# First part of an expert begun inside the last attention blocks, and the last chunk routed block by block

## The chip, the cores and the metric

One core of a Trainium2 chip runs the kernel. The metric is the device time of one execution in microseconds (us); the kernel before has a median of 445.17 us over 3 runs. The engines are PE (TensorE, matrix products), DVE (VectorE), ACT (ScalarE), POOL (GpSimd) and SP (SyncE, which issues transfers). Each works through its own instructions in the order in which the program wrote them.

## The reference

The input is attention with a decaying state (4 batches, 8 heads, 768 steps, width 48), and its output goes through a layer of 8 experts, of which each token takes one:

```python
y[:, :, t] = einsum('bhd,bhde->bhe', rt, state + cur)      # cur = outer(u * kt, vt)
state = wt[:, :, :, None] * state + einsum('bhd,bhe->bhde', kt, vt)
x = y.transpose(0, 2, 1, 3).reshape(3072, 384)
expert_idx = argmax(x @ w_gate);  gate_w = softmax(x @ w_gate)[expert_idx]
for e in range(8):
    out[mask] = gate_w[mask, None] * (maximum(x[mask] @ w1[e], 0) @ w2[e])
```

## The kernel before, in words

**Attention.** The sequence is cut into 6 chunks of 128 steps, and chunk c of batch b is block n = 4c + b, so there are 24 blocks, 0 to 23. `iteration(n)` (L692) does for block n the products `pe_a` (k against r, tile `ap`), `pe_inter` (the state's part, into `yp`) and `pe_av` (values, into `yp`), prepares block n + 2 on DVE and ACT (`dve_suf`, `dve_kh`, `dve_pre`, `dve_rh`, `pe_coef`, `pe_coef_tr`) and finishes block n - 1 (`act_y`, `pe_y`, `act_xr`, which leave its rows in `xr`). `pe_coef` and `pe_state` begin with a few products of zeros, `keep_warm` (L108), whose results nobody reads; blocks 20 to 23 have no `pe_state`, and iterations 22 and 23 no `pe_coef`.

**Routing.** The logits of a chunk are computed, `gate` (L521, five small DVE operations) finds the expert, `count` adds up how many tokens each expert has, `rank` (L565, three small products for one block) and `place` (L581, three DVE operations) give each token its row, `weigh` the factor, and `scatter` (L647) is an indirect transfer on POOL's queue that stores the rows by expert in DRAM. Chunks 0 to 4 are routed whole, four blocks at a time, one chunk later. In the last chunk each block is routed alone (`pe_logits`, L596): its logits one iteration after its attention, gate at the end of that iteration, rank and place in the one behind it. `rank` of block n - 2 stands on PE between `pe_a(n)` and `pe_inter(n)` (L711).

**Experts.** An expert takes its rows (`load_rows`), transposes them (`transpose_rows`, L265), and for 8 groups f computes `expand` (L273: 9 products into a bank, then `hh` by ACT and `hl` by DVE), and then `contract` or the products of L872, 24 for each output tile. Expert 0 goes in two parts: `pa`, 192 rows that come from chunks 0 to 3 and are thus there early, and `pb`, 256 rows, whose load waits for every scatter. In the kernel before `pa` is loaded at the end of iteration 20, transposed at the end of iteration 22, its group 0 stands in iteration 23, and groups 1 to 7 behind, with the routing of blocks 22 and 23 between them. Then come `pa.mm2(0)`, `pb.trans`, `pa.mm2(1)`, the 8 groups of `pb` and the other experts.

**What sets the order.** It is written out by hand for PE, DVE, ACT and POOL (`manual_schedule`, L888), and for SP too. PSUM tiles come in rings: `psX` has 2 buffers (transposes, `rank`, and in the kernel before the single-block logits), `psL` 1 (`pe_coef`, `pe_coef_tr`), `psK` and `psA` 2 each. A new tile waits until those who read the tile two (or one) before it are done. `transpose_rows` takes three `psX` tiles, each read by ACT and then by DVE:

```python
for j in range(3):
    pt = psX.tile([P, nq * rows], F32, name="pt", tag="tp")
    ...
    nc.scalar.activation(xh[:, j, :], pt, AF.Copy)
    nc.vector.tensor_tensor(out=xl[:, j, :], in0=pt, in1=xh[:, j, :].bitcast(F32), op=ALU.subtract)
```

Of the kernel before, what the change touches and what calls it, by code (L numbers as in the profile page):

```python
# [19 lines left out]
P = 128  # L20
C = 128
NCH = S // C
# [23 lines left out]
def rwkv_moe_kernel(ctx, tc, rkw, vv, ub, wgp, wg, w1, w2, out):  # L46
# [192 lines left out]
    def scatter_out(t, q, rows):  # L239
# [3 lines left out]
        for k in outs:  # L243
# [1 line left out]
        outs.append(i.ins)  # L245

    banks = [(psK, "kp"), (psK, "kp"), (psY, "yp"), (psL, "lg")]
    htags = [("suf", "pre"), ("suf", "pre"), ("rk", "rk"), ("rk", "rk"), ("kh", "rh"), ("kh", "rh"), ("kh", "rh"),
             ("kt", "kt"), ("at",), ("at",)]
    nth = {"b": 0, "h": 0}  # L250

# [28 lines left out]
        nc.scalar.activation(hh, hp, AF.Relu)  # L280
        nc.vector.scalar_tensor_tensor(out=hl, in0=hp, scalar=0.0, in1=hh.bitcast(F32), op0=ALU.max, op1=ALU.subtract)  # L281

    def contract(wt, hs, q, rows, t):
        op = psA.tile([rows, DM], F32, name="opt", tag="ap")
        i = 0
        for f in range(8):
            hh, hl = hs[f]
            cs = slice(q * rows, (q + 1) * rows)
            for a, w in ((hh, "h"), (hl, "h"), (hh, "l")):
                nc.tensor.matmul(op, a[:, cs], w2v(wt, w, f), start=(i == 0), stop=(i == 23))  # L290
                i += 1
        o = ld.tile([rows, DM], F32, name="ort", tag="vt")
        nc.vector.tensor_scalar(out=o, in0=op, scalar1=t[:, q, DM:DM + 1], scalar2=None, op0=ALU.mult)
        scatter_out(t, q, o)
# [203 lines left out]
    def pe_y(n):  # L498
        if real(n):
            yq = psX.tile([P, NP_ * RP], F32, name="yq", tag="tp")  # L500
            for q in range(NP_):
                nc.tensor.transpose(yq[:, q * RP:(q + 1) * RP], blk[n]["yt"][:, q, :], ident[:RP, :RP])  # L502
            blk[n]["yq"] = yq
# [33 lines left out]
    def act_ex(k):  # L537
        ex = sm.tile([P, B, E], F32, name="ex", tag="ex")[:, 0:k[2]]
        nc.scalar.activation(ex, ch["r", k][0], AF.Exp)
        ch["ex", k] = ex  # L540
# [14 lines left out]
    def weigh(k):  # L555
        c, b, m = k
        se = sm.tile([P, B], F32, name="se", tag="se")[:, 0:m]
        nc.vector.tensor_reduce(out=se, in_=ch["ex", k], axis=AX.X, op=ALU.add)
        nc.vector.tensor_scalar(out=se, in0=se, scalar1=1e-9, scalar2=None, op0=ALU.add)
        nc.vector.reciprocal(ch["xr", c][:, b:b + m, DM], se)  # L560
# [4 lines left out]
    def rank(k):  # L565
        c, b, m = k
        oh = ch["r", k][1]
        oa = ch["old", k]
        rk = psX.tile([P, B + 1, E], F32, name="rank", tag="tp")
        ch["rank", k] = rk  # L570
        if c == ROUTED:
            nc.tensor.matmul(rk[:, B, :], ones, oa, start=True, stop=True, skip_group_check=True)
        rk = rk[:, 0:m, :]
        nc.tensor.matmul(rk, tri, oh, start=True, stop=False, skip_group_check=True)
        nc.tensor.matmul(rk, ones[0:1, :], ebrow[:, 0:m], start=False, stop=False, skip_group_check=True)
        nc.tensor.matmul(rk, ones, oa.unsqueeze(1).broadcast_to([P, m, E]), start=False, stop=(m == 1), skip_group_check=True)
        for i in range(m - 1):
            nc.tensor.matmul(rk[:, i + 1:m, :], ones, oh[:, i:i + 1, :].broadcast_to([P, m - 1 - i, E]),
                             start=False, stop=(i == m - 2), skip_group_check=True)
# [16 lines left out]
    def pe_logits(n):  # L596

        c, b = divmod(n, B)
        lg = psX.tile([P, 1, E], F32, name="lg", tag="tp")
        for q in range(NP_):  # L600
            nc.tensor.matmul(lg[:, 0, :], blk[n]["yt"][:, q, :], wgt[:, q, 0:E], start=(q == 0), stop=(q == NP_ - 1))
        ch["lp", (c, b, 1)] = lg
# [59 lines left out]
    class Part:  # L662
# [13 lines left out]
            expand(wt0, f, self.x[0], self.x[1], bank(2 * self.rows), hh, hl)  # L676
            self.hs.append((hh, hl))

        def mm2(self, q):
            contract(wt0, self.hs, q, self.rows, self.t)  # L680

    load_v(0)
    for n in range(1, LD):
# [8 lines left out]
    def iteration(n):  # L692

        c, b = divmod(n, B)
        route = c - 1 if n >= 0 else -1
        if n >= 0:
            load(n + 6)
            load_v(n + 5)
        last = c == NCH - 1
        whole = (route, 0, B)  # L700
        act_y(n - 1)
        pe_a(n)
        dve_suf(n + 2)
        act_g(n + 1)
        if route >= 0 and b == 1:
            act_ex(whole)
        pool_rk(n + 3)
        if n in (6, 7):
            scatter(0, (2 * n - 12,))
        if last and b > 1:  # L710
            rank((c, b - 2, 1))  # L711
        pe_inter(n)
        dve_at(n)
        dve_state(n - 1)
        pool_diag(n + 1)
        act_diag(n + 1)
        if n in (6, 7):
            scatter(0, (2 * n - 11,))
        if route > 0 and b > 1:
            scatter(route, (2 * b - 4, 2 * b - 3))  # L720
        if route >= 0 and b == 1:
            count(whole)
            weigh(whole)
        if n > 0 and b == 1:
            ch["xr", c] = xrp.tile([P, B, XC], F32, name="xr", tag="xr")
            pool_ids(c)
        if last and b > 1:
            act_ex((c, b - 2, 1))
            place((c, b - 2, 1))
            weigh((c, b - 2, 1))  # L730
        if last and b == 3:
            scatter(c, (0,))
        pe_y(n - 1)
        if last and b > 0:
            pe_logits(n - 1)
        if n == NB - 1:
            pa.mm1(0)
        dve_kh(n + 2)
        act_xr(n - 1)
        pe_coef(n + 2)  # L740
        act_cs(n + 2)
        if route >= 0 and b == 0:
            logit_mm(route)
        if route >= 0 and b == 1:
            rank(whole)
        pe_kt(n + 1)
        act_kt(n + 1)
        dve_pre(n + 2)
        if route >= 0 and b == 0:
            logit_tr(route)  # L750
        pe_state(n)
        pe_coef_tr(n + 2)
        act_ct(n + 2)
        act_wt(n + 2)
        dve_rh(n + 2)
        for k in lows:
            split_piece(*k, half="l")
        lows.clear()
        if route >= 0 and b == 0:
            gate(whole)  # L760
        if route >= 0 and b == 1:
            place(whole)
        if last and b > 0:
            gate((c, b - 1, 1))
            count((c, b - 1, 1))
        act_junk(n + 2)
        m = n - 8
        if 0 <= m < 12:
            lows.append((wt0, stg[0, m // 3], m // 3, 3, m % 3))
            split_piece(*lows[0], half="h")  # L770
        pe_av(n)
        if n == NB - 2:
            pa.trans()
        if n == 0:
            zero_rows()
        if n == 1:
            late_constants()
        if 1 <= n < 5:
            prefill(2 * n - 2)
            prefill(2 * n - 1)  # L780
        if n in (6, 9, 12, 15):
            stg[0, n // 3 - 2] = load_piece(one, n // 3 - 2)
        if n in (14, 17, 20, 21):
            stg[1, (14, 17, 20, 21).index(n)] = load_piece(SECOND, (14, 17, 20, 21).index(n))
# [101 lines left out]

    ET = mybir.EngineType
    with tc.manual_schedule(engines={ET.PE, ET.DVE, ET.Activation, ET.Pool}):  # L888
        for n in range(-3, NB):
            iteration(n)  # L890
            if n == 20:
                pa = Part(0, HA // 2)
                full, banks = banks, banks[0:2]

        nl = NB - 1
        mid, end = (NCH - 1, B - 2, 1), (NCH - 1, B - 1, 1)
        act_y(nl)
        banks = [(psA, "ap"), (psA, "ap"), (psK, "kp"), (psK, "kp")]
        pa.mm1(1)
        rank(mid)  # L900
        act_ex(mid)
        place(mid)
        weigh(mid)
        pe_y(nl)
        pe_logits(nl)
        scatter(NCH - 1, (1, 2))
        act_xr(nl)
        gate(end)
        act_ex(end)
        count(end)  # L910
        pa.mm1(2)
        pa.mm1(3)
        rank(end)
        place(end)
        weigh(end)
        scatter(NCH - 1, (3,))
        pa.mm1(4)
        sort_experts()
        check_w()
        pa.mm1(5)  # L920
        pa.mm1(6)
        check()
        actx.close()
        wpb = mctx.enter_context(tc.tile_pool(name="wpb", bufs=1))
        wts.append(weight_tiles(wpb))
        pa.mm1(7)
        split_piece(wts[1], stg[1, 0], 0)
        pb = Part(HA, HB // 2)
        load_x(1)
        expert(2)  # L930
        feed(1, 0, False)
        pa.mm2(0)
        pb.trans()
        split_piece(wts[1], stg[1, 1], 1)
        feed(1, 1, False)
        pa.mm2(1)
        banks = full
        nth["b"] = 0
        for f in range(8):
            pb.mm1(f)  # L940
            if f in (1, 4):
                feed(1, 2 + f // 4)
        pb.mm2(0)
        trans_x(1)
        pb.mm2(1)
# [203 lines left out]
```

## Time and profile before

| what | us |
|---|---|
| median of 3 runs (lowest, highest) | 445.17 (444.72, 447.03) |
| the profiled execution | 448.3 |
| its span, first to last instruction | 446.6 |
| PE busy | 420.1 (94%) |
| DVE, ACT, POOL busy | 285.4, 223.4, 125.5 |

The mean granted TensorE clock is 0.966 of full speed. All times below are from the span's start. A timeline's line gives start, length, engine, line and operation, out<-in tiles, sizes and, in brackets, how long the engine stood idle before it and what ended that. PE's lengths overlap a little, so what a group of products costs is read from one start to the next, as the chain of waits does.

### The profile page before, as it was taken

The numbers are of one execution on the slowest core, as the hardware profiler recorded it, in microseconds if no ns is written. First come the engines' busy times: TensorE is split into PE (matmuls) and PEld (weight loads), VectorE is DVE, ScalarE is ACT, GpSimd is POOL, SyncE is SP. The second block draws the span as 40 slices with busy tenths as digits, with TensorE's granted clock in tenths as the row PEclk, the third lists the DMA queues.
The fourth block names the chain that finished last, engine by engine and source line by source line (L and its number), as shares of the span: only waits on it lengthen the run. The fifth ranks groups of instructions, "written<-read, shape, count | busy, mean of one in ns | idle before, by whom it ended". The sixth has DMA issues, their size and how long they took to land.

```text
span 446.6 us, 9684 instructions
## 1 busy us (share of the span) xinstructions
PE 420.1 (94%) x3662; PEld 368.4 (82%) x3663; DVE 285.4 (64%) x554; ACT 223.4 (50%) x625; POOL 125.5 (28%) x159
## 2 busy tenths in 40 slices
PE   8989999999899979998999999999999999999990
PEld 6557778777677758897999988899999999999990
DVE  5899899999999994374875166165363572722310
ACT  3678787787786861232755244353353461522200
POOL 3663255451634523011010012022030080210710
PEclk9999999999999995598999999999999999999997
DMA  7999977776863152036572643544365335000120
GB/s 201 215 216 285 240 208 197 192 238 130 253 170 107 57 169 90 19 101 189 156 243 66 198 133 93 174 149 116 133 189 161 114 89 160 27 26 1 23 59 23
DMA packets 33179, 62.61 MB, mean 140 GB/s; under 512 B 8086, under 2 KB 21199, under 8 KB 33126
## 3 DMA queue, kind: packets, MB, share of 16 engines
q1 hardware_dynamic: 25222, 52.41, 42.4%
q0 software_dynamic: 7904, 9.52, 6.9%
q8 instruction: 30, 0.49, 0.5%
q14 instruction: 23, 0.19, 0.1%
HBM read 50.03 MB, written 12.29 MB: 140 GB/s over the span
## 4 chain that ended last, share of the span: by engine, by line
issue 38%; PE 33%; DVE 11%; ACT 6%; POOL 5%; DMA 3%; POOLq 0%; ACTq 0%; DVEq 0%
PE bank L278 7%; POOL out_dram L240 4%; DMA out_dram<-ot,xg 3%; PE bank L872 3%; PE opt L290 3%; PE yp L473 3%; PE wrm L111 2%; DVE at L364 2%; PE yp L495 2%; PE ap L461 2%; DVE pre L356 2%; DVE suf L340 2%; PE dp L486 2%; PE yq L502 2%; ACT junk L379 1%
## 5 line engine op out<-in xcount | busy, mean ns | idle before, releaser
L240 POOL DMA_INDIRECT out_dram<-ot,xg x24 | 35.3, 1470 | 156.9 <-DVE ot L862 151.4
L216 DVE TENSOR_TENSOR w2l<-wst,w2h 128x512 fp32r<-128x512 f32 x48 | 31.4, 685 | 44.6 <-ACT w2h L214 44.1
L278 PE MATMUL bank<-xl,w1h 128*128 128x448 f32 (+6 forms) x168 | 59.0, 355 | 0.0
L278 PE MATMUL bank<-xh,w1l 128*128 128x448 f32 (+6 forms) x168 | 58.2, 352 | 0.0
L278 PE MATMUL bank<-xh,w1h 128*128 128x448 f32 (+6 forms) x168 | 55.7, 359 | 0.4 <-issue 0.3
L312 POOL TENSOR_TENSOR rk<-rkwt 112x512 f32<-112x512 f32 x24 | 33.6, 1399 | 76.1 <-DVE pre L344 55.4
L281 DVE SCALAR_TENSOR_TENSOR hl<-bank,hh 128x192 fp32r<-128x192 f32 (+8 forms) x58 | 30.4, 539 | 32.4 <-ACT hh L280 32.2
L280 ACT ACTIVATE hh<-bank 128x192 fp32r<-128x192 f32 (+8 forms) x58 | 26.6, 477 | 46.7 <-PE bank L278 43.9
L872 PE MATMUL bank<-hl,w2h 128*128 128x412 f32 (+5 forms) x114 | 40.6, 358 | 0.0
L872 PE MATMUL bank<-hh,w2l 128*128 128x412 f32 (+5 forms) x114 | 40.5, 357 | 0.0
L877 ACT ACTIVATE oT<-bank 128x448 f32<-128x448 f32 (+5 forms) x18 | 9.4, 525 | 61.6 <-PE bank L872 61.6
L872 PE MATMUL bank<-hh,w2h 128*128 128x412 f32 (+5 forms) x114 | 39.9, 356 | 0.0
L650 POOL DMA_INDIRECT xs<-xr,pi x24 | 26.2, 1091 | 28.1 <-DVE sh L527 11.5
L364 DVE COPY_PREDICATED at<-cmask,ap 128x512 f32<-128x512 int32 x48 | 32.3, 727 | 2.7 <-PE ap L461 2.2
L340 DVE TENSOR_TENSOR_SCAN suf<-rkwt,sufone 112x520 f32<-112x520 f32 x24 | 31.1, 1296 | 4.2 <-DMA rkwt<-in_rkw_dram 4.2
L278 PEld LDWEIGHTS bank<-xh,w1h 128*128 128x128 f32 x168 | 31.2, 188 | 1.9 <-issue 0.5
L278 PEld LDWEIGHTS bank<-xl,w1h 128*128 128x128 f32 x168 | 31.6, 188 | 1.1
L278 PEld LDWEIGHTS bank<-xh,w1l 128*128 128x128 f32 x168 | 31.5, 188 | 1.1
L214 ACT ACTIVATE w1h<-wst 128x512 fp32r<-128x512 f32 x48 | 28.2, 628 | 8.1 <-PE bank L278 7.9
L216 DVE TENSOR_TENSOR w1l<-wst,w1h 128x512 fp32r<-128x512 f32 x48 | 30.9, 685 | 1.2 <-PE bank L278 0.6
L356 DVE TENSOR_TENSOR_SCAN pre<-rkwt,pre 112x520 f32<-112x520 f32 x24 | 31.1, 1295 | 0.0
L334 ACT ACTIVATE at<-ident,ct 128x128 f32<-128x128 f32 x96 | 30.5, 391 | 0.1
(163 smaller groups left out, 932.1 us busy)
## 6 DMA issues: line engine op xcount, KB each, us to landing
wst<-in_w_dram SPq DMA_DIRECT2D x48, 256.0 KB, 3.8
wst<-in_w_dram SPq DMA_DIRECT2D x16, 768.0 KB, 6.9
rkwt<-in_rkw_dram SPq DMA_DIRECT2D x36, 289.5 KB, 6.6
vt<-in_vv_dram SPq DMA_DIRECT2D x24, 192.0 KB, 5.7
rkwt<-in_rkw_dram SPq DMA_DIRECT2D x5, 675.5 KB, 16.8
xg<-xs SPq DMA_DIRECT2D x5, 579.0 KB, 4.4
xs<-zrow SPq DMA_DIRECT2D x8, 289.5 KB, 6.8
xg<-xs SPq DMA_DIRECT2D x2, 675.5 KB
```

What stands on the lines that cost most here:

```text
L214: nc.scalar.activation(hi, st[:, cs], AF.Copy)
L216: nc.vector.tensor_tensor(out=lo, in0=st[:, cs], in1=hi.bitcast(F32), op=ALU.subtract)
L240: i = nc.gpsimd.indirect_dma_start(out=out[:, :], out_offset=bass.IndirectOffsetOnAxis(ap=t.bitcast(I32)[:, q, DM + 1:DM + 2], axis=0), in ...
L278: nc.tensor.matmul(hp, a, x[:, j, :], start=(i == 0), stop=(i == 8))
L280: nc.scalar.activation(hh, hp, AF.Relu)
L281: nc.vector.scalar_tensor_tensor(out=hl, in0=hp, scalar=0.0, in1=hh.bitcast(F32), op0=ALU.max, op1=ALU.subtract)
L312: i = nc.gpsimd.tensor_tensor(out=d["rk"], in0=d["r"], in1=d["k"], op=ALU.mult)
L334: nc.scalar.activation(blk[n]["at"][:, 1, q], ident, AF.Copy, scale=blk[n]["ct"][:, 2 * q + 1:2 * q + 2])
L340: nc.vector.tensor_tensor_scan(out=suf[:, ::-1], data0=d["w"][:, ::-1], data1=sufone.rearrange("p q c -> p (q c)")[:, ::-1], initial=0.0, ...
L356: nc.vector.tensor_tensor_scan(out=pre, data0=d["w"], data1=pre0[n % 2].rearrange("p q c -> p (q c)"), initial=0.0, op0=ALU.mult, op1=ALU.add)
L364: nc.vector.copy_predicated(out=d["at"][:, j], mask=cmask.unsqueeze(1).broadcast_to([P, NP_, C]), data=d["ap"][j])
L872: nc.tensor.matmul(pp, w, a, start=(i == 0), stop=(i == 23))
```

## The change

The loop ends with iteration 21, and the last two blocks are written out. `pa` is loaded at the end of iteration 19 and transposed in iteration 21; its groups 0 and 1 stand in block 22's iteration, 2 and 3 in block 23's, and 4 to 7 behind. Each block of the last chunk is gated later: block 20 behind `dve_at(22)` and no longer at the end of iteration 21, block 21 behind `dve_at(23)`, blocks 22 and 23 behind groups 4 and 5 of `pa`. The single-block logits use `psL` in place of `psX`. `pb.trans` moves into `pa.mm2(1)`, behind 15 of its 24 products. The order of the tiles that hold `hh` and `hl` is turned round to match.

```diff
-    def contract(wt, hs, q, rows, t):
+    def contract(wt, hs, q, rows, t, between=None):
...
+            if f == 4 and between is not None:
+                between()
...
-        lg = psX.tile([P, 1, E], F32, name="lg", tag="tp")
+        lg = psL.tile([P, 1, E], F32, name="lg", tag="lg")
...
         pe_y(n - 1)
-        if last and b > 0:
-            pe_logits(n - 1)
-        if n == NB - 1:
-            pa.mm1(0)
+        act_xr(n - 1)
+        if last and b == 1:
+            pa.trans()
         dve_kh(n + 2)
-        act_xr(n - 1)
...
-        if route >= 0 and b == 1:
+        if route >= 0 and b == 1 and not last:
             place(whole)
-        if last and b > 0:
-            gate((c, b - 1, 1))
-            count((c, b - 1, 1))
+        if last and b == 1:
+            pe_logits(n - 1)
...
-        for n in range(-3, NB):
+        for n in range(-3, NB - 2):
             iteration(n)
-            if n == 20:
+            if n == NB - 5:
                 pa = Part(0, HA // 2)
...
+        n = NB - 2
+        act_y(n - 1)
+        pe_a(n)
+        act_g(n + 1)
+        pe_inter(n)
+        dve_at(n)
+        pool_diag(n + 1)
+        act_diag(n + 1)
+        place(before)
+        scatter(lc - 1, (0, 1))
+        gate(one_of[0])
+        act_ex(one_of[0])
+        count(one_of[0])
+        pa.mm1(0)
+        pe_y(n - 1)
+        act_xr(n - 1)
+        pe_logits(n - 1)
+        pa.mm1(1)
+        rank(one_of[0])
+        weigh(one_of[0])
+        pe_av(n)
+        n = NB - 1
+        act_y(n - 1)
+        pe_a(n)
+        pe_inter(n)
+        dve_at(n)
+        scatter(lc - 1, (2, 3))
+        place(one_of[0])
+        scatter(lc, (0,))
+        gate(one_of[1])
+        act_ex(one_of[1])
+        count(one_of[1])
+        weigh(one_of[1])
+        pa.mm1(2)
+        pe_y(n - 1)
+        act_xr(n - 1)
+        pe_logits(n - 1)
+        rank(one_of[1])
+        pa.mm1(3)
+        pe_av(n)
+        act_y(n)
         banks = [(psA, "ap"), (psA, "ap"), (psK, "kp"), (psK, "kp")]
...
         pa.mm1(4)
+        place(one_of[1])
+        scatter(lc, (1,))
+        gate(one_of[2])
+        act_ex(one_of[2])
+        count(one_of[2])
+        weigh(one_of[2])
+        rank(one_of[2])
+        pe_y(n)
+        pe_logits(n)
+        place(one_of[2])
+        scatter(lc, (2,))
+        act_xr(n)
+        pa.mm1(5)
+        gate(one_of[3])
+        act_ex(one_of[3])
+        count(one_of[3])
+        rank(one_of[3])
+        pa.mm1(6)
+        place(one_of[3])
+        weigh(one_of[3])
+        scatter(lc, (3,))
         sort_experts()
         check_w()
-        pa.mm1(5)
-        pa.mm1(6)
+        pa.mm1(7)
         check()
...
         pa.mm2(0)
-        pb.trans()
+        pa.mm2(1, pb.trans)
...
-        pa.mm2(1)
```

## Rows read from the trace of the kernel before

**Rows 1.** What PE waited for, 210 to 446 us: total, times, longest.

```profile
PE bank L278 <- issue: 0.3, 1, 0.3
```

**Rows 2.** Busy time by stretch (PE, PEld, DVE, ACT, POOL), granted PE clock, DMA share, GB/s.

```profile
164.10:167.10 3.00, 0.01 (x1) 0.01 (x1) 2.73 (x12) 1.81 (x7) 0.66 (x1) 1.00 0.50 174
167.80:187.50 19.70, 19.20 (x128) 16.81 (x124) 6.79 (x32) 3.50 (x11) 5.25 (x10) 0.50 0.16 61
201.30:204.20 2.90, 0.86 (x7) 0.63 (x7) 1.30 (x3) 0.66 (x2) 0.94 (x1) 1.00 1.00 260
205.00:208.00 3.00, 3.00 (x11) 2.56 (x11) 2.20 (x4) 1.41 (x3) 0.00 (x0) 0.50 0.13 49
```

**Rows 3.** Timeline of PE in iterations 21 and 22.

```profile
159.65 0.65 PE L111 MATMUL cp<-wz,ones 128*128 128x384 bf16 x3
...
161.05 0.39 PE L444 MATMUL cpt<-pick,cs 128*128 128x8 f32 x2
...
162.93 1.16 PE L461 MATMUL ap<-rh,kh 64*128 64x128 f32 x16
167.09 0.18 PE L574 MATMUL rank<-oh,tri 128*128 128x8 bf16 x1 [3.00 <-DVE oh L533]
```

**Rows 4.** Timeline of POOL: a scatter of chunk 3, and the last scatter.

```profile
150.34 0.98 POOL L650 DMA_INDIRECT xs<-xr,pi  x1 [0.21 <-issue]
...
194.70 0.97 POOL L650 DMA_INDIRECT xs<-xr,pi  x1 [2.98 <-DVE ks L611]
```

**Rows 5.** Timeline of PE from the last rank to the first group of `pb`.

```profile
192.09 0.18 PE L574 MATMUL rank<-oh,tri 128*128 128x8 bf16 x1
...
202.62 0.66 PE L269 MATMUL pt<-ident,xg 128*128 128x128 f32 x4 [1.35 <-DMA xg<-xs]
...
204.19 0.41 PE L290 MATMUL opt<-w2h,hh 128*96 128x384 f32 x1
...
210.01 0.40 PE L278 MATMUL bank<-x,w1h 128*128 128x256 f32 x2
```

**Rows 6.** Timeline of ACT.

```profile
159.94 0.52 ACT L412 ACTIVATE xr<-yq 128x192 f32<-128x192 f32 x2
...
161.54 0.18 ACT L423 ACTIVATE ct<-cpt 128x8 f32<-128x8 f32 x1 [0.54 <-PE cpt L444]
...
184.50 0.33 ACT L280 ACTIVATE hh<-bank 128x192 fp32r<-128x192 f32 x1 [7.88 <-PE bank L278]
```

**Rows 7.** Timeline of DVE.

```profile
162.50 0.18 DVE L560 RECIPROCAL xr<-se 128x4 f32<-128x4 f32 x1
...
184.86 0.36 DVE L281 SCALAR_TENSOR_TENSOR hl<-bank,hh 128x192 fp32r<-128x192 f32 x1 [4.87 <-ACT hh L280]
...
185.92 0.17 DVE L533 SCALAR_TENSOR_TENSOR oh<-ix,iom 128x8 bf16<-128x8 f32 x1
```

**Rows 8.** Chain of waits (start, us, what), PE's pieces at the full clock.

```profile
155.34 1.01 PE yp L495 x16
156.35 1.09 PE ap L461 x16
...
158.46 0.53 PE yq L502 x4
158.99 0.81 PE lg L601 x8
...
190.16 2.10 PE bank L278 x18
...
424.56 11.16 PE opt L290 x64
```

**Rows 9.** The same chain, PE's pieces at half the clock.

```profile
175.66 2.01 PE ap L461 x16
...
184.46 1.88 PE yp L495 x16
186.34 1.89 PE bank L278 x9
```

More of the change, by code (lines that the diff above doesn't have):

```diff
@@ L247, in rwkv_moe_kernel @@
     banks = [(psK, "kp"), (psK, "kp"), (psY, "yp"), (psL, "lg")]
-    htags = [("suf", "pre"), ("suf", "pre"), ("rk", "rk"), ("rk", "rk"), ("kh", "rh"), ("kh", "rh"), ("kh", "rh"),
+    htags = [("rk", "rk"), ("rk", "rk"), ("suf", "pre"), ("suf", "pre"), ("kh", "rh"), ("kh", "rh"), ("kh", "rh"),
              ("kt", "kt"), ("at",), ("at",)]
@@ L677, in mm1, with mm2 @@
             self.hs.append((hh, hl))
-        def mm2(self, q):
-            contract(wt0, self.hs, q, self.rows, self.t)
+        def mm2(self, q, between=None):
+            contract(wt0, self.hs, q, self.rows, self.t, between)
     load_v(0)
@@ L709, in iteration @@
             scatter(0, (2 * n - 12,))
-        if last and b > 1:
-            rank((c, b - 2, 1))
         pe_inter(n)
@@ L726, in iteration @@
             pool_ids(c)
[L727 to L732, printed above, removed]
         pe_y(n - 1)
-        if last and b > 0:
-            pe_logits(n - 1)
-        if n == NB - 1:
-            pa.mm1(0)
+        act_xr(n - 1)
+        if last and b == 1:
+            pa.trans()
         dve_kh(n + 2)
-        act_xr(n - 1)
         pe_coef(n + 2)
@@ L771, in iteration @@
         pe_av(n)
-        if n == NB - 2:
-            pa.trans()
         if n == 0:
@@ L888, in rwkv_moe_kernel @@
     with tc.manual_schedule(engines={ET.PE, ET.DVE, ET.Activation, ET.Pool}):
-        for n in range(-3, NB):
+        for n in range(-3, NB - 2):
             iteration(n)
-            if n == 20:
+            if n == NB - 5:
                 pa = Part(0, HA // 2)
[L893 to L897, printed above, removed]
-        banks = [(psA, "ap"), (psA, "ap"), (psK, "kp"), (psK, "kp")]
-        pa.mm1(1)
@@ L900, in rwkv_moe_kernel @@
[L900 to L916, printed above, removed]
-        pa.mm1(4)
+        lc = NCH - 1
+        one_of = [(lc, b, 1) for b in range(B)]
+        before = (lc - 1, 0, B)
+        full, banks = banks, banks[0:2]
@@ L925, in rwkv_moe_kernel @@
         wts.append(weight_tiles(wpb))
-        pa.mm1(7)
         split_piece(wts[1], stg[1, 0], 0)
```

## The prediction, made before the run

> **What bounds the kernel now.** I read the busy shares first: PE works in 94% of the span, so the question is where PE stands still and where its clock is low. The list of PE's waits from 210 us on shows 0.3 us in all [rows 1]: behind the first group of `pb`, at 210.01 us [rows 5], PE never waits for anybody, and whatever the change gains or loses before that point goes to the end of the kernel one for one. The forecast is therefore one number: when does that group start after the change?
>
> Before that point the stretches with their granted clock [rows 2] show the weak place. PE does nothing from 164.10 to 167.10, because `rank` of block 20 waits for `oh` with `pe_inter(22)` queued behind it [rows 3]; right after that the clock is 0.50, 1.2 GHz, and stays there from 167.8 to 187.5 although PE is busy in 19.20 of these 19.70 us. It came back while `pe_av(23)` and a group of `pa` ran back to back. A second fall follows 201.30 to 204.20, where PE was busy 0.86 us and otherwise waited for the rows of `pb` and for its transposes, and lasted through the stretch 205 to 208, in which PE was busy all the time with long products. At half clock a piece takes 1.8 to 1.9 times as long: `ap` 2.01 against 1.09, `av` 1.88 against 1.01, a group of nine 1.89 against 1.05 [rows 8, 9].
>
> **The change, part by part.** Groups are called m0 to m7.
>
> *The earlier load of `pa`.* It is issued behind the scatters of chunk 3, the last at 150.34 [rows 4]. The last scatter of all, at 194.70, was followed by load and first transpose at 202.62 [rows 4, 5], 7.9 us later, a bound from above; 150.34 + 7.9 = 158.3, before PE wants the rows at 158.99, behind `pe_y(20)` [rows 8]. Cost 0. The two weight loads behind it on SP's queue wait for buffers that are freed later, so they lose nothing.
>
> *The transposes in iteration 21.* This is the first cost. `psX` has two buffers. The first pair starts at 158.99. The second takes the buffer of `pe_y(20)`, which ACT reads until 159.94 + 0.52 = 160.46 [rows 6]: PE stands 1.2 us. The third takes the buffer of the first, which DVE must have read; that subtraction is queued behind `weigh`, which ends at 162.66 [rows 7], and takes 0.36 (the same shape as `hl`): PE may go on at 163.05, another 2.25 us idle. A pair is about 0.3 us (an estimate: half of two pieces like `yq`), so 163.35. Then `pe_coef` and the chunk's rank, 1.40 us from 159.65 to 161.05, then `cpt` and ACT's copy, 0.67 from 161.05 to 161.72 [rows 3, 6], because the logits now share the one `psL` buffer: 165.4. Logits 0.81 and `av` 1.01 [rows 8]: `pe_a(22)` starts at 167.25, where it had started at 162.93 [rows 3], 4.3 us late. DVE's work for block 23 moves back by 1.5 us and is covered: PE wants it an iteration later.
>
> *Iterations 22 and 23.* The wait of 3.00 us goes, since gate now has the whole first half of iteration 22. At the full clock one iteration is ap 1.09, inter 1.01 (as `av`), m 1.05, `yq` 0.53, logits 0.81, m 1.05, rank 0.36 (three products, 0.12 apart), av 1.01: 6.9 us, two of them 13.8. So `av(23)` ends at 181.1 with four groups done; before, it ended at 184.46 + 1.88 = 186.34 [rows 9] with one. `place` of chunk 4 and its scatters, now later on DVE and POOL, lie beside this: nobody reads these rows before `pb`.
>
> *Behind `av(23)`.* This is the second cost: the order puts `gate` behind an expand group on DVE, and `rank` in front of all else on PE. After m4 PE has only `rank` of block 22, and waits for `hh` (0.36 to the start of `hl`), `hl` 0.27 to the next start [rows 6, 7], `place` 0.6 (three operations at 0.2) and `gate` 1.0 (from the end of `hl` at 185.22 to that of `oh` at 186.09, and 0.1 between engines): 2.35. `pe_y(23)` and the logits could run but stand behind it. The same after m5 without `place`: 1.75. So m4 1.05 + 2.35 + rank, `yq`, logits 1.70 + m5 1.05 + 1.75 + rank 0.36 + m6 1.05 = 9.3, that is 190.4. From the end of the group ahead of the last `place` to the last scatter it was 2.6 us (192.09 to 194.70) and then 7.9 to the transposes: 200.9. PE's own work until then, m7 and 39 products at 0.174 [rows 8], is 7.8 and lies under these 10.5; the 2.7 us of PE that this leaves are first the check of the weights, then the load.
>
> *`pb.trans` inside `mm2(1)`.* From the first transpose to the next product it was 1.57 us (202.62 to 204.19) [rows 5]; nine products are left, 1.57 us. The first group of `pb` starts at 204.0, and 0.3 for five more hand-overs between engines: 204.3, **5.7 us earlier, if the clock stays full throughout.** DVE's later splitting of weights beside `pb` is hidden: there are four banks and PE has 4 us before it meets the first.
>
> *The clock.* In iteration 21 PE would stand 3.4 of the 4.1 us up to 163.05, and the time between m4 and m5 is 4.05 us with 1.7 of small pieces, followed by 1.75 of nothing. Both resemble 201.30 to 204.20 (0.86 of 2.90 busy), behind which the clock fell. A fall costs between nothing and 10 us (half of the 20 us of the first). For the first I take the logits, `av` and `ap` at half clock, 0.7 + 0.87 + 0.92 = 2.5, since then `av(21)`, `pe_a`, `pe_inter` and m0 run without a wait, like the products that brought it back before. For the second I take the logits, m5 and m6: 0.7 + 0.84 + 0.84 = 2.4; m7 at half clock is hidden under the load of `pb`. Together 4.9: the first group of `pb` at 209.2, **0.8 us earlier**.
>
> One rule speaks against this placing of the transposes. No row here shows transposes alone; the six records before the second fall [rows 2, 5] come mixed with waits. The Trainium skill, page "TensorE: Matmul & The Clock Gate", Part 4, says that a transpose on TensorE does not count as work in the same way and that the full clock doesn't engage for it. By that rule iteration 21 falls as in the sum (209.2); without it that stretch might hold, and the sum would be 206.7.
>
> **The sum.** The profiled execution took 448.3 us, 446.6 of span and 1.7 around it; minus 0.8 is 447.5. The median shown is 445.17, 3.1 below, and I take the difference over to it: 444.4 us. About 0.5%, 2.2 us, is what a measurement of this kernel can tell from no change, so this counts as the same.
>
> **The rivals.**
> - *Only one of the two falls happens.* Then 3.2 to 3.3 us are gained: 441.9. For it: between the two waits of the second stretch stand 1.7 us of pieces and the whole of m5, more than stood between the waits in front of either fall of before [rows 2]. Against: each stretch alone has as much idle time as those had. With no fall at all 5.7 are gained, 439.5.
> - *The clock does not come back in iteration 22.* One place, the products behind the transposes. In the kernel before, `ap`, `rank`, `inter` of block 23 at 175 to 180 did not bring it back, nor did m0. If the whole of iteration 22 runs at half clock, each of its pieces costs its difference: 0.92 + 0.88 + 0.84 + 0.41 + 0.7 + 0.84 + 0.87 = 5.5 us more, hence 3.8 later than before instead of 0.8 earlier (the 0.92 of `ap` is already in): 449.0. If block 23 goes the same way it is 9.3 later, 454.5. It decides against the change once the clock is still 0.50 beyond about 173 us.
> - *The timed runs of before had a shorter slow stretch than the profiled one.* Then the 3.1 us between 448.3 and 445.17 are part of what the change could save, and it saves them only once: 447.5, slower by 2.3. For it: half of a stretch of 6 us would be just that. Against: a profile may simply take longer.
> - *The change doesn't do what it says*, because the rows of `pa` land later than 158.99. At worst PE stands some 2 us longer in iteration 21, which the order hides nowhere: 446.4. The margin of 0.7 us speaks against it.
>
> **How the numbers follow.** Forecast 0.38. One fall 0.22 and none 0.06: faster 0.28. Clock not back in iteration 22 0.17 (of this 0.07 for the longer form) and the shorter stretch of before 0.15: slower 0.32. Late rows 0.02, with the forecast: same 0.40. The forecast's own range is 443.2 to 446.6, from 0.3 us in each of the four chained waits down and 2.2 us of a longer fall up. The whole range, 441.0 to 449.5, leaves out no fall at all and the longer form of the second rival, 0.13, and some of the edges.
>
> **What would show it.** Right: two idle stretches of PE at 159 to 163 in front of the second and third transpose pairs, ended by ACT and DVE; no wait at `rank` of block 20; waits of about 2.4 and 1.8 us in front of the ranks of blocks 22 and 23, ended by DVE's `oh`; half clock for some 7 us from about 164 and again from about 187; the last scatter at 196 to 199 and the first group of `pb` near 209. Wrong: that group before 207 (a fall missing), or after 211 (the clock low through iteration 22), or PE waits behind `pb`, which would say that the gain was handed to another engine.

## The result, and the profile after the change

The change made the kernel slower. The median is 450.57 us (448.01 to 457.44, 20 runs) against 445.04 us (443.5 to 447.51, 20 runs) before; the ratio is 1.0118 with a 95% interval from 1.0093 to 1.0144. The forecast was 444.4 with a range to 449.5, so the measured time lies outside it, and on the other side of no change. Ratios, here and below, leave out executions more than 1.5% above the fastest of their kernel, and medians do not, so that a ratio need not be the quotient of two medians. The profiled execution took 457.44 us, the longest of the 20, with a mean granted clock of 0.948 against 0.960 in the median. By these figures an execution at the median has some 11 us less of half clock than the one shown here (an estimate: twice what the clock lacks to 1, times the span).

PE's busy share and its clock in that execution, by fortieths of the span:

```profile
PE   8989999999899969968999999999999999999990
...
PEclk9989999999999965867999999999999999999997
```

What PE waited for between 150 and 220 us (total, times, longest), to be read beside the single wait of 3.00 us in [rows 3]:

```profile
PE rank L576 <- DVE oh L535: 3.9, 2, 2.2
PE pt L269 <- DVE x L271: 2.8, 2, 2.1
PE pt L269 <- ACT xr L414: 1.5, 1, 1.5
PE ng L634 <- DVE gb L629: 1.0, 1, 1.0
```

All the waits that the forecast had named are there, with their sizes: 1.5 and 2.1 in front of the second and third transposes (forecast 1.2 and 2.25), 2.2 and 1.7 at the ranks of blocks 22 and 23 (forecast 2.35 and 1.75). The wait at the rank of block 20 is gone. The timeline of PE shows where they stand:

```profile
160.27 0.38 PE L269 MATMUL pt<-ident,xg 96*128 96x96 f32 x2 [0.28 <-DVE sh L529]
162.13 0.39 PE L269 MATMUL pt<-ident,xg 96*128 96x96 f32 x2 [1.47 <-ACT xr L414]
164.59 0.58 PE L269 MATMUL pt<-ident,xg 96*128 96x96 f32 x2 [2.08 <-DVE x L271]
...
171.72 2.08 PE L463 MATMUL ap<-rh,kh 64*128 64x128 f32 x16
...
195.54 0.17 PE L576 MATMUL rank<-oh,tri 128*128 128x8 bf16 x1 [2.23 <-DVE oh L535]
...
201.27 0.17 PE L576 MATMUL rank<-oh,tri 128*128 128x8 bf16 x1 [1.68 <-DVE oh L535]
...
206.88 0.19 PE L634 MATMUL ng<-gb,ones 112*128 112x1 bf16 x1 [1.03 <-DVE gb L629]
...
215.31 0.60 PE L269 MATMUL pt<-ident,xg 128*128 128x128 f32 x4
...
218.48 0.40 PE L278 MATMUL bank<-x,w1h 128*128 128x256 f32 x2
```

The last line is the first group of `pb`: 218.48, where it was 210.01 [rows 5]. The wait of 1.35 us for the rows of `pb` is gone too. What grew is the clock's part, as the busy time by stretch shows (PE, PEld, DVE, ACT, POOL, granted clock, DMA share, GB/s):

```profile
160.00:164.60 4.60, 0.78 (x5) 0.41 (x5) 4.33 (x15) 2.37 (x9) 0.00 (x0) 0.77 0.76 247
164.60:186.40 21.80, 21.47 (x145) 18.48 (x147) 6.81 (x22) 6.26 (x21) 4.89 (x9) 0.50 0.16 57
186.40:193.20 6.80, 6.80 (x74) 6.25 (x74) 3.60 (x16) 1.91 (x6) 1.05 (x2) 1.00 0.09 31
193.20:195.50 2.30, 0.11 (x1) 0.00 (x0) 1.55 (x10) 0.54 (x2) 0.19 (x1) 1.00 0.00 0
196.70:206.90 10.20, 7.49 (x37) 7.00 (x37) 3.70 (x24) 1.46 (x6) 1.75 (x3) 0.50 0.10 39
206.90:210.30 3.40, 3.40 (x12) 2.97 (x13) 1.79 (x12) 1.27 (x3) 0.34 (x2) 0.50 0.25 71
```

PE stands still in two places, and after each the clock is 0.50 (1.2 GHz). The first time the half clock lasts 24 us, from 162.5 to 186.4, 2.1 of them in the stretch to 164.6, whose mean is 0.77; behind it PE is busy 21.47 of 21.80 us and the clock stays down. The second time it lasts 13.6 us, until 210.3. In [rows 2] it was about 20 us and 3 us.

### The profile page after: what moved, and what is told of

Its sections match the earlier page's. It is cut to its first block, busy times and chain, and to the rows that moved or that the text cites. A ratio compares the mean times of both kernels' runs of the same rounds, so it can differ in the third digit from the quotient of the medians.

```text
span 455.7 us, 9682 instructions
## 1 busy us (share of the span) xinstructions
PE 425.3 (93%) x3663; PEld 373.2 (82%) x3663; DVE 283.0 (62%) x554; ACT 223.8 (49%) x625; POOL 125.9 (28%) x159
## 4 chain that ended last, share of the span: by engine, by line
issue 36%; PE 31%; DVE 15%; ACT 6%; POOL 5%; DMA 4%; SPq 0%; POOLq 0%; ACTq 0%
PE bank L278 8%; POOL out_dram L240 4%; DMA out_dram<-ot,xg 3%; PE bank L861 3%; PE opt L290 3%; DVE suf L342 3%; DVE at L366 3%; PE yp L497 2%; PE wrm L111 2%; DVE pre L358 2%; ACT at L336 2%; PE ap L463 2%; DVE kh L352 2%; PE dp L488 2%; PE dp L111 1%
## 5 line engine op out<-in xcount | busy, mean ns | idle before, releaser
L314 POOL TENSOR_TENSOR rk<-rkwt 112x512 f32<-112x512 f32 x24 | 32.5, 1355 | 78.1 <-DVE pre L346 52.8
L463 PE MATMUL ap<-rh,kh 64*128 64x128 f32 (+1 forms) x384 | 30.5, 303 | 0.0
```

The source lines that it names most:

```text
L314: i = nc.gpsimd.tensor_tensor(out=d["rk"], in0=d["r"], in1=d["k"], op=ALU.mult)
L463: nc.tensor.matmul(d["ap"][j][:, q, :], d["kh"][rs, q, :], d["rh"][rs, q, :], start=True, stop=True)
```

## The experiments

Two theories stood against each other. **Clock theory:** the loss is the half clock that follows the waits. **Wait theory:** the loss is the waits themselves, and the clock is a side effect. All runs were timed beside the kernel before, which took 445.18 us beside the first four kernels below (a_fill to a_both), 445.91 beside b_fill, b_between, b_best and a_nobetween, and 444.93 beside the other four. Medians of the mean granted clock are given with the times; the kernel before has 0.968, the changed one 0.960.

**a_fill: work into the waits, nothing else.** The products of zeros are read by nobody; the first edit is in `transpose_rows` and holds for `pa` alone.

```diff
+            if fill is not None and j < 2:
+                keep_warm(fill, (6, 9)[j])
...
+        keep_warm(warm_bank(), 9)
         rank(one_of[2])
...
+        keep_warm(warm_bank(), 7)
         rank(one_of[3])
```

> The changed kernel with products of zeros put into four of its PE waits (6 and 9 of them behind the first and second transposes of iteration 21, 9 and 7 ahead of the ranks of blocks 22 and 23); every wait and every order of work stays. Clock theory (the loss is the half clock that follows these waits): the granted clock stays full from 159 to the first group of pb, that group starts near 205 to 207 in the place of 218, and the median goes from 450.6 to 439 to 443. Wait theory (the loss is the waits themselves): nothing is gained, 449 to 452.

Measured: 443.7 us, ratio to before 0.9941 (0.9904 to 0.9978), clock 0.988. Busy time by stretch of this kernel:

```profile
159.00:164.00 5.00, 4.68 (x24) 2.06 (x24) 4.25 (x14) 2.61 (x10) 0.00 (x0) 1.00 0.86 275
164.00:186.00 22.00, 21.39 (x236) 18.25 (x235) 12.59 (x53) 8.60 (x31) 6.98 (x13) 1.00 0.15 56
186.00:193.30 7.30, 5.54 (x42) 4.24 (x41) 3.30 (x22) 1.32 (x5) 1.31 (x3) 1.00 0.14 54
193.30:196.70 3.40, 2.99 (x10) 2.64 (x11) 1.81 (x14) 0.90 (x2) 0.78 (x2) 0.50 0.16 58
```

The same delays, now filled, and the clock stays full from 159 to 193; `pb` begins at 205.16. The one fall left follows a wait that was not filled, 2.0 us at the check of the weights. So 6.9 us of the changed kernel (450.57 to 443.7) are clock alone, more than all that it lost against before. The wait theory falls as the whole explanation. The clock is not the whole of the difference either, since the kernel before has half clock of its own: with that filled and mended (b_fill_psk below, also at 0.988) it takes 439.2 us, 4.5 less than a_fill, in which all the waits of the changed kernel are still there. The median came out 0.7 above the expected range; the executions lie between 439.72 us and 450.35 us, the last with a clock of 0.971.

**a_psk: the waits at the transposes taken away** (`spare` is true for `pa` alone).

```diff
-            pt = psX.tile([P, nq * rows], F32, name="pt", tag="tp")
+            pool, tag = (psX, "tp") if j == 2 or not spare else (psK, "kp")
+            pt = pool.tile([P, nq * rows], F32, name="pt", tag=tag)
```

> The changed kernel with the first two transposes of iteration 21 in psK, which is idle there, in the place of psX: the waits of 1.5 and 2.1 us for psX go, the waits at the ranks of blocks 22 and 23 stay. Clock theory: the first stretch of half clock (162.5 to 186.4) goes or is much shorter, the second stays; 443 to 446. Wait theory: only the 3.6 us of waits are gained, 447.

Measured: 444.72 us, ratio 0.9971 (0.9945 to 0.9997), clock 0.968. 5.9 us are gained, more than the 3.6 of the waits and inside the clock theory's range:

```profile
161.10:167.90 6.80, 6.47 (x46) 5.76 (x48) 4.59 (x13) 3.33 (x13) 0.63 (x1) 0.50 0.44 159
168.00:184.90 16.90, 14.67 (x166) 13.45 (x162) 9.37 (x49) 4.99 (x17) 6.34 (x12) 1.00 0.16 59
185.00:198.60 13.60, 10.90 (x47) 9.95 (x47) 5.80 (x36) 2.89 (x8) 2.09 (x4) 0.50 0.16 49
```

The first stretch is 6.8 us long, the second, behind the ranks, lasts 13.6 us as in the changed kernel.

**a_gate: the waits at the ranks taken away.**

```diff
-        pa.mm1(4)
         place(one_of[1])
...
         weigh(one_of[2])
+        pa.mm1(4)
         rank(one_of[2])
...
-        pa.mm1(5)
         gate(one_of[3])
         act_ex(one_of[3])
         count(one_of[3])
+        pa.mm1(5)
         rank(one_of[3])
-        pa.mm1(6)
         place(one_of[3])
         weigh(one_of[3])
+        pa.mm1(6)
```

> The changed kernel with the gates of blocks 22 and 23 put ahead of groups 4 and 5 (and the last place ahead of group 6): the waits of 2.2 and 1.7 us at the ranks go, the transposes of iteration 21 stay as they are. Clock theory: the second stretch of half clock (196.7 to 210.3) goes, the first stays; 3.9 us of waits and 2 to 4 of clock, 443 to 445. Wait theory: 3.9 us alone, 446.7.

Measured: 441.62 us, ratio 0.9914 (0.9882 to 0.9946), clock 0.974. 9.0 us are gained, 5 more than the waits; the median lies 1.4 us below the clock theory's range and 5 below the wait theory's value:

```profile
158.00:161.20 3.20, 0.56 (x4) 0.20 (x2) 3.10 (x8) 2.14 (x8) 0.00 (x0) 1.00 0.82 228
161.20:171.40 10.20, 8.97 (x64) 6.99 (x66) 3.85 (x10) 3.63 (x14) 0.64 (x1) 0.50 0.24 85
171.50:201.60 30.10, 28.22 (x256) 25.75 (x254) 18.23 (x90) 10.18 (x30) 9.40 (x17) 1.00 0.36 121
```

The second stretch is gone altogether. And with everything up to `av(23)` in the very order of the changed kernel, the first lasts 10.2 us here and 24 us there: how long it lasts differs between executions. Here the clock is back in `pe_inter(22)`, the second of these lines:

```profile
169.24 2.08 PE L463 MATMUL ap<-rh,kh 64*128 64x128 f32 x16
171.25 1.17 PE L475 MATMUL yp<-rh,gbd 64*64 64x128 f32 x16
```

In the profile of a_nobetween (454.85 us), with the same order up to there, the first stretch lasts about 11 us, from 158.0 to 168.9, and ends in `pe_inter(22)` too; the clock then falls again behind a new wait, of which more below.

**a_both: both edits.**

> Both edits, transposes in psK and gates ahead of the groups. Clock theory: full clock from 159 on, pb's first group near 201 to 203, 436 to 440, better than both kernels. Wait theory: 7.5 us of waits, 443.

Measured: 435.62 us, ratio 0.9768 (0.9736 to 0.9801), clock 0.987. The gains add up: 5.9 + 9.0 = 14.9, measured 15.0 from 450.57, twice the 7.5 us of the waits themselves. This version beats both kernels. The median lies 0.4 below the expected range, but not for the reason expected: the profile still has two short falls, and `pb` begins at 198.89 all the same, ahead of the 201 to 203 that were put down for a full clock:

```profile
163.10:166.50 3.40, 3.40 (x32) 2.87 (x28) 2.85 (x4) 1.84 (x7) 0.70 (x1) 0.50 0.32 106
166.50:183.50 17.00, 16.96 (x186) 15.53 (x184) 10.65 (x55) 6.09 (x21) 7.42 (x14) 1.00 0.19 71
183.60:190.40 6.80, 6.66 (x29) 6.04 (x28) 4.24 (x29) 1.65 (x4) 1.05 (x2) 0.50 0.28 94
```

The second fall follows no wait: PE was busy in 16.96 of the 17.00 us ahead of it. In a_gate, with the same order in that place, the clock held from 171.5 to 201.6. So waits are not the only thing behind which the clock falls; what brought this fall was not found.

**b_fill: the kernel before, its wait of 3.0 us filled.**

```diff
         if last and b > 1:
+            if b == 2:
+                keep_warm(psK.tile([P, BANK], F32, name="wrm", tag="kp"), 13)
             rank((c, b - 2, 1))
```

> The kernel before with 13 products of zeros in front of the rank of block 20, in the wait of 3.0 us that was there; nothing else is touched. Clock theory: the half clock from 167 to 187 does not come, and at 0.4 to 0.5 us for each us of it the median goes from 445 to 435 to 438. Wait theory: no change, 444 to 446.

Measured: 446.66 us, ratio 1.0 (0.9966 to 1.0034), clock 0.975. The clock theory missed by 9 us, and no change is what the wait theory had expected. PE's timeline shows what the clock theory had left out:

```profile
162.51 2.98 PE L111 MATMUL wrm<-wz,ones 128*128 128x512 bf16 x13
...
169.28 0.39 PE L269 MATMUL pt<-ident,xg 96*128 96x96 f32 x2
171.16 0.36 PE L269 MATMUL pt<-ident,xg 96*128 96x96 f32 x2 [1.50 <-DVE sh L527]
172.97 0.58 PE L269 MATMUL pt<-ident,xg 96*128 96x96 f32 x2 [1.45 <-DVE x L271]
```

The wait had only been the first of a chain. With PE ahead, the transposes of iteration 22 wait 3.0 us for `psX`, the same ring that cost the changed kernel its first fall; before, at half the clock, the wait there was 0.5 us. The clock falls at 171.7 in place of 167.3. The profiled execution is the fastest of the 12 (442.84); for the median there is only an estimate: a clock of 0.975 in place of 0.968 is some 6 us less of half clock, worth about 3 us, and the new waits take nearly as much.

**b_fill_psk: that second wait taken away as well** (the edit of b_fill and that of a_psk, on the kernel before).

> The kernel before with the 13 products of zeros in the wait of 3.0 us and with the first two transposes of pa in psK, so that the waits of 1.5 and 1.5 us, into which the filled wait had only moved, go too. Clock theory: now the half clock of iterations 22 and 23 does not come (mean granted clock 0.985 or more in the place of 0.967), 438 to 441. If the clock falls all the same, for want of products in these two iterations, 443 to 446: then the groups of pa between the blocks are what keeps it.

Measured: 439.2 us, ratio 0.9886 (0.9826 to 0.9946), clock 0.988. In the profiled execution, the fastest of the six, the clock stays full throughout:

```profile
161.00:165.00 4.00, 3.84 (x32) 2.22 (x30) 3.79 (x11) 2.87 (x10) 0.89 (x2) 1.00 0.78 231
165.00:198.70 33.70, 30.44 (x264) 26.84 (x263) 20.27 (x89) 10.74 (x31) 9.19 (x17) 1.00 0.33 109
```

So the clock of the kernel before can be held without moving any group of `pa`, and that is worth 5.7 us, although the wait of 3.0 us is still there, filled: this is clock and hardly wait. It is not held in every execution: two of the six took 444.77 and 451.37 us, with a clock of 0.978 and 0.959.

**b_between, b_best, b_all, a_nobetween: the move of `pb.trans`.** b_between is the kernel before with `pa.mm2(1, pb.trans)` alone; b_best has b_fill's edit too, b_all also the transposes in `psK`; a_nobetween is the changed kernel with the move undone.

> The kernel before with the transposes of pb inside the second contraction of pa, behind 15 products, and no other part of the change. If this part of the change is worth what the trace of before shows (1.35 us of waiting for the rows of pb, and 1.7 us for the fall of the clock behind it): 442 to 443.5. If the rows are the limit wherever the transposes stand: 444.5 to 445.5.

> Both edits to the kernel before. Clock theory: they add up, 432.5 to 436, as fast as the mended changed kernel (435.6), which would say that beginning pa earlier buys nothing that the clock does not. If beginning pa earlier has a worth of its own, this stays 2 us or more behind 435.6.

> The same with the transposes of pb inside the second contraction of pa. Against the changed kernel with its two waits mended (435.6), which has all of this and four groups of pa between the blocks: 435 to 437 if the clock is all that the early groups give, 438 to 444 if they have a worth of their own.

> The changed kernel with the transposes of pb back between the two contractions of pa. Rows of pb landed some 2 us after the first contraction ended, so PE would wait 2 to 2.6 us there and the clock may fall once more: 452.5 to 455. If that part of the change does nothing: 449.5 to 451.5.

Measured: b_between 444.26 us, 0.9954 (0.993 to 0.9979); b_best 445.98, 0.9983 (0.9949 to 1.0017); b_all 440.96, 0.9898 (0.9855 to 0.994); a_nobetween 452.32, 1.0129 (1.0089 to 1.0169), beside 1.0118 for the changed kernel. The transposes of `pb` in b_between and in a_nobetween:

```profile
202.86 0.60 PE L269 MATMUL pt<-ident,xg 128*128 128x128 f32 x4
```

```profile
209.35 0.66 PE L269 MATMUL pt<-ident,xg 128*128 128x128 f32 x4 [0.74 <-DMA xg<-xs]
```

The wait for the rows is gone in the first and there, with 0.74 us, in the second. On the kernel before the move is worth 1.7 us (445.91 to 444.26), between the two expectations. On the changed kernel its loss does not show: 1.0129 and 1.0118 lie within each other's intervals, though the median is 1.8 us higher; it lies between the two expectations. On top of b_fill the move gains 0.7 and on top of b_fill_psk it loses 1.8 (439.2 to 440.96); neither shows, as the intervals overlap. b_best stays far behind the 432.5 to 436 of the clock theory for the reason that b_fill did.

b_all is 5 us behind a_both: each against the kernel before, 0.9898 and 0.9768 with intervals apart. That would say that beginning `pa` earlier has a worth of its own, but the clock is not the same in the two, 0.980 against 0.987. Up to the first contraction the order of b_all is that of b_fill_psk, and still the clock fell in its profile, as `pe_inter(23)` shows, first in b_fill_psk, then in b_all:

```profile
173.46 1.08 PE L474 MATMUL yp<-rh,gbd 64*64 64x128 f32 x16 [0.48 <-ACT ytb L401]
```

```profile
176.86 1.97 PE L476 MATMUL yp<-rh,gbd 64*64 64x128 f32 x16 [0.44 <-ACT ytb L403]
```

`pb` begins at 205.59 there, and in the profile of b_fill_psk, at full clock, at 198.75, as early as in a_both, whose profile has 10 us of half clock. Executions of b_all and a_both with the same mean clock are nearer to a fair comparison: 439.66, 439.97 and 440.2 us against 436.84, 436.08 and 435.39 us at 0.982, 0.984 and 0.985. These 3 to 5 us speak for a worth of the early groups; no run shows it with the clock held in both.

**a_both_psx and a_both_warm: small edits to a_both.** The first gives `pe_logits` back to `psX`, the second has 6 in place of 3 products of zeros in `pe_coef` of block 23.

> The mended changed kernel (435.6) with the single-block logits back in psX, as before the change: they need not wait for the copy of cpt in iteration 21 (0.3 us), but the ring of psX gets longer waits behind place and gate. If psL is where the change loses something, 434 to 435; if psL was needed, 437 to 441.

> The mended changed kernel (435.6) with 6 in place of 3 products of zeros in pe_coef of block 23, 0.5 us of PE work under the wait of 0.6 us at the chunk's rank behind it. If the fall of the clock in iteration 21 that is left (3.4 us) still costs something: 434 to 435.3. If the products cost what they save: 435.3 to 436.3.

Measured: 445.02 us, 0.9935 (0.9889 to 0.9981), clock 0.967; and 440.28, 0.9868 (0.9817 to 0.992), clock 0.979. Both lie above all that was expected of them. With `psX` the logits wait 1.8 us for DVE's reading of the transposes, which speaks for `psL`, and the wait told of below is in that profile too. In iteration 21 of a_both_warm the clock holds, but PE then waits in a new place:

```profile
170.74 1.16 PE L464 MATMUL ap<-rh,kh 64*128 64x128 f32 x16
173.78 1.08 PE L476 MATMUL yp<-rh,gbd 64*64 64x128 f32 x16 [1.88 <-ACT ytb L403]
```

The clock falls at 175 behind it. ACT's copy began at 173.13, 2.3 us after `av(22)` had ended by the records, with ACT idle. DVE's copy of `ap` began as late, at 173.34, so it may be PE's products that ended later than their records say. A wait of this size at `pe_inter` also stands in the profiles of a_nobetween (1.8) and a_both_psx (1.7), and in no other. What holds up the engines there was not found.

## Why the prediction was wrong, step by step

**The waits: right.** Those at the transposes and at the ranks came where they were put, each within 0.3 us, and a_fill, in which the clock hardly falls, has `pb` at 205.16 where the sum for a full clock said 204.3; the 2.0 us at the check of the weights, which the forecast had put under the load of `pb`, are most of the rest. (The terms that the forecast lists for the waits at the ranks add up to 2.23 and 1.63, not to 2.35 and 1.75; 2.23 and 1.68 were measured.)

**The first step that failed: the price of the first half clock.** The forecast gave it 2.5 us, for the logits, `av` and `ap`, "since then `av(21)`, `pe_a`, `pe_inter` and m0 run without a wait, like the products that brought it back before". It was wrong in two ways. The clock fell at 162.5, ahead of `pe_coef`, the rank and `cpt`, whose half clock the forecast had put at nothing. And in the profiled execution it was still 0.50 through m0, m1 and both blocks' `pe_a`, and back at 186.4; this is the shorter form of the second rival, iteration 22 at half clock, with `pe_a(23)` besides. That `pb` came at 218.48, near the 219.3 of the longer form, is luck.

Leg by leg against the forecast's 209.2: from `pe_y(20)`'s end to `pe_a(22)` 11.8 us in place of 9.8, of which 1.0 is the half clock from `pe_coef` to `cpt`; from there to the end of `av(23)` 20.3 in place of 14.7; from there to the end of m6 11.5 in place of 11.7; from there to `pb` 14.9 in place of 13.9, because m7 and the first contraction ran at half clock until 210.3 and PE waited 1.0 us at the check of the weights, so that what the load of `pb` was to hide took 11.8 us and the load was reckoned at 10.5. The rest is 0.9 us by which this execution was late at 159 already.

The leg of 20.3 us belongs to long executions. In a_gate the first leg is 11.8 us as well, but the clock is back in `pe_inter(22)`, as the forecast had it. With some 11 us less of half clock than the profiled execution, one at the median would have about 12 us in the first stretch (an estimate), near the 10.2 of a_gate and the 11 of a_nobetween; the forecast had some 7 us. Over the 20 executions of the changed kernel the time goes with the granted clock, from 0.966 at 448.01 to 0.948 at 457.44.

**The second step that failed: the base.** The forecast took its 0.8 us off the median 445.17 and gave the shorter slow stretch of the timed runs 0.15. What lies between the first group of `pb` and the time of the same execution is nearly constant: 448.3 - 210.01 = 238.3 before, 239.0 after, 237.7 in a_fill, 238.6 in b_between, 239.2 in a_gate, and 237.4 to 239.6 over all the profiles. So a median of 445.04 means a start of `pb` near 206.6 (an estimate, good to about 1 us), not at 210.0: the profiled execution of before was a long one, and 209.2 + 238.4 is 447.6. Of the 6.2 us between 444.4 and 450.57, 3.2 are this base. The first leg (2.0 too short), the third (0.2 too long) and the fourth (1.0 too short) give 2.8 of the other 3.0, if the clock of an execution at the median is back in `pe_inter(22)`; no profile of this kernel shows that. Among the rivals the third, 447.5, had the base right, and the second the clock of long executions; its 449.0 is nearest in number, but stands on the wrong base as well.

**The second half clock: right in place, too small by 1 us** (the fourth leg: m7, the check of the weights and the first contraction). a_gate removes it whole.

**The transposes between the products of `mm2(1)`: right.** The wait for the rows went, alone on the kernel before (1.7 us) as in the whole change.

**The rule on transposes: not settled.** The clock fell at iteration 21's transposes with waits (changed kernel, a_gate) and with only short ones behind them (a_psk: 0.6 and 0.3 us), but in b_fill_psk, with the same transposes a block later and without waits for a buffer, it held; in b_all, the same order up to there, it fell at 176, some 3 us behind them. No run has transposes alone. The Trainium skill, "TensorE: Matmul & The Clock Gate", Part 4, says that the full clock does not engage for a transpose, which does not count as work in the same way. The runs here neither bear this out nor contradict it.

## What to carry to other kernels

When work is moved into gaps, list for each moved piece what it must wait for on every engine: here the transposes brought waits for a two-buffer PSUM ring and a busy DVE, and a gate queued behind an expand's copy brought a wait that the order before had avoided. Then ask what the clock does behind each new wait, from the wait itself on and not from the next long product, and look for idle buffers (here `psK`) before filling with empty work. And carry a forecast over to the timed runs from an absolute point in the profile plus a constant rest, not as a difference to a single profiled execution.

## What was not expected

Filling a wait of 3.0 us in the kernel before gained nothing, because half the clock had hidden the next wait. PE busy 21.47 of 21.80 us did not bring the clock back, while in a_psk it was back after 6.8 us; and in a_both the clock fell behind 17 us without a wait. One order of instructions gave 10.2, 11 and 24 us of half clock in the profiles of three kernels that share it, and the time of the changed kernel spreads over 9 us (448.01 to 457.44), against 4 before.
